# Attention with a distance bias and a two-layer network behind it: from stages with a bias matmul to one written order with a band multiply

## The chip, the core and the metric

One core of a Trainium2 chip. The metric is device time of one execution in microseconds, the median of the runs.

## What is computed

```python
scores = q @ k^T / 8 + bias_table[bucket(|i - j|)]      # 8 batches x 8 heads, 576 x 576, head size 64
attn = softmax(scores)                                  # over j
x = (attn @ v), heads side by side                      # 4608 tokens x 512
h = max(x @ w_in, 0)                                    # 512 -> 2048
out = (h * h) @ w_out                                   # 2048 -> 512
```

All inputs and the output are f32. The bucket of a distance is the distance itself below 16, grows with its logarithm from there, and is 31, the last one, from 128 on.

## The kernel before

The work runs in stages: the attention of two batches, then both layers for their 1152 tokens (`ffn`), four times. An automatic scheduler orders the instructions within what the data allow; all PSUM tiles come from one pool of four tiles of two banks.

`attention_batch` first transposes Q and K of a batch on TensorE in f32, five pieces for each pair of heads (`transpose_pair`, L162 and L165); VectorE copies them to bf16 and scales Q (L171, L173). VectorE casts V to f16 into a tile with a 65th column of 1/64 (L191 to L199), so that the row sums come out of the same matmul as the values.

The scores stand transposed: keys on the partitions, queries along the columns, in blocks of 128 keys (the fifth has 64) and 288 queries. A block gets two matmuls. The first adds the bias (L213): a reversed identity of 128 x 128 times a window of `dbuf_sb`, a table in which each partition holds the bias by distance, shifted by one (built over DRAM at the start, L129 to L144). The second adds K^T Q with the 64 rows of one head (L222). ScalarE takes the exponential of both query halves, 576 columns, to f16 (L231). Then come 10 matmuls for a head with the weights as moving operand (L241). To divide by the row sum, ScalarE takes its logarithm (L251), GpSimd spreads it over 64 partitions (L256), ScalarE takes exp(-x) (L257), and VectorE multiplies (L255, L260).

`ffn` computes layer 1 in 16 blocks of 128 hidden columns, 12 matmuls each (L277), ScalarE rectifies (L284), VectorE squares (L291). Layer 2 takes 9 token blocks of 16 matmuls of 512 columns (L297); VectorE scales them out of PSUM (L305) and SP writes them out. All loads are issued on SP's queue, those of the next batch after the casts of this one.

Of the kernel before, what the change touches and what calls it, by code (L numbers as in the profile page):

```python
# [19 lines left out]
NJT = 5  # L21
VSC = 1.0 / 64.0
OSC = 1.0 / 4096.0
EXPF = mybir.ActivationFunctionType.Exp
RELUF = mybir.ActivationFunctionType.Relu
MULT = mybir.AluOpType.mult


def _rel_bucket_diag():
    t = np.arange(1151)  # L30
    n = np.abs(t - 575)
    half = NBK // 2
    max_distance = 128
    is_small = n < half
# [5 lines left out]
    return np.where(is_small, n, large).astype(np.int64)  # L40
# [3 lines left out]
def kernel(  # L44
# [10 lines left out]
    nc = tc.nc  # L55

    bidx = _rel_bucket_diag()
    oh = np.zeros((NBK, 1280), dtype=np.float32)
    uu = np.arange(128, 128 + 1151)
    oh[bidx, uu] = 1.0  # L60
    oh_d = nc.inline_tensor(oh, name="c_oh")
    revi_d = nc.inline_tensor(
        np.eye(128, dtype=np.float32)[::-1].astype(ml_dtypes.bfloat16), name="c_revi"
    )
    id_d = nc.inline_tensor(np.eye(128, dtype=np.float32), name="c_id")
    dfull_dram = nc.dram_tensor("t_dfull", (H, 1280), BF16, kind="Internal")

    single = ctx.enter_context(tc.tile_pool(name="single", bufs=1))
    et_pool = ctx.enter_context(tc.tile_pool(name="et", bufs=12))
    qk_pool = ctx.enter_context(tc.tile_pool(name="qk", bufs=8))  # L70
    v1_pool = ctx.enter_context(tc.tile_pool(name="v1", bufs=2))
    st_pool = ctx.enter_context(tc.tile_pool(name="stg", bufs=1))
    ws_pool = ctx.enter_context(tc.tile_pool(name="ws", bufs=1))
    xt_pool = ctx.enter_context(tc.tile_pool(name="xt", bufs=2))
    sm_pool = ctx.enter_context(tc.tile_pool(name="sm", bufs=3))
    ff_pool = ctx.enter_context(tc.tile_pool(name="ff", bufs=1))
    ps = ctx.enter_context(tc.tile_pool(name="ps", bufs=4, space=bass.MemoryType.PSUM))

    id_sb = single.tile([128, 128], FP32, name="id_sb")
    revi_sb = single.tile([128, 128], BF16, name="revi_sb")  # L80
    dbuf_sb = single.tile([128, H, 1152], BF16, name="dbuf_sb")
    w_in_sb = single.tile([128, 4, 2048], FP16, name="w_in_sb")
    w_out_sb = single.tile([128, 16, 512], FP16, name="w_out_sb")
    bt_sb = single.tile([32, 16], FP32, name="bt_sb")
    gt_sb = ff_pool.tile([128, 16, 1152], FP16, name="gt_sb")

    stgs = {}

    def load_sdh(src, b, tag):
        stg = st_pool.tile([128, NJT, 512], FP32, tag=tag, name=tag)  # L90
        for tt in range(4):
            nc.sync.dma_start(
                out=stg[:, tt, :].rearrange("p (h d) -> p h d", h=8),
                in_=src[b, :, ts(tt, 128), :].transpose([1, 0, 2]),
            )
# [251 lines left out]
```

## Time and profile before

| | before |
|---|---|
| runs, us | 659.6, 654.64, 655.17 (median 655.17) |
| span of the profiled execution, first to last instruction, us | 652.9 |
| median less that span, us | 2.3 |
| TensorE, ScalarE, VectorE, GpSimd busy, us | 619.2, 342.7, 235.3, 60.6 |
| bytes read and written in HBM, MB | 39.32, 9.46 |

The profile shows one execution. Busy times are unions of instruction intervals; ends of matmuls are modelled, so distances between their starts say more than their lengths. L-numbers are lines of the kernel printed above.

### The profile page before, as it was taken

What the parts mean: (1) busy time and instruction counts of PE and PEld (TensorE: products, weight loads), DVE (VectorE), ACT (ScalarE), POOL (GpSimd) and SP (SyncE); (2) the same over time, 40 slices, a digit from 0 to 9 for tenths busy, and PEclk for the clock granted to TensorE, in tenths of its full rate; (3) what the DMA queues carried; (4) which work ended last, traced back from release to release, by engine and by line L of the source; (5) the groups of instructions that cost most, each with busy time, mean ns of one, the idle gap of its engine ahead of it and who ended that gap; (6) DMA issues with size and microseconds to landing.
All of it is one profiled execution on the core that took longest, in us unless ns stands there. A gap on an engine that the chain in (4) does not pass through costs nothing.

```text
span 652.9 us, 8868 instructions
## 1 busy us (share of the span) xinstructions
PE 619.2 (95%) x3590; PEld 296.4 (45%) x3590; DVE 235.3 (36%) x327; ACT 342.7 (52%) x581; POOL 60.6 (9%) x76
## 2 busy tenths in 40 slices
PE   6699989899999999999999999989999999999997
PEld 3244534454454444445454454445445445444543
DVE  2223644642243262433142352343324325324321
ACT  0188688561038758665007757846202785876500
POOL 0021121100002211200001211210000211220000
PEclk9999999999999999999999999989999999999999
DMA  7992767341180091030227038000016300000012
GB/s 168 252 211 89 229 206 177 73 74 48 65 167 11 1 180 41 0 73 1 81 80 130 1 69 150 1 2 2 32 67 139 53 1 1 2 0 1 1 65 81
DMA packets 122169, 49.36 MB, mean 76 GB/s; under 512 B 113768, under 2 KB 113896, under 8 KB 121616
## 3 DMA queue, kind: packets, MB, share of 16 engines
q1 hardware_dynamic: 122128, 48.79, 33.0%
q8 instruction: 28, 0.46, 0.3%
q14 instruction: 13, 0.11, 0.1%
HBM read 39.32 MB, written 9.46 MB: 75 GB/s over the span
## 4 chain that ended last, share of the span: by engine, by line
PE 52%; issue 30%; ACT 9%; POOL 3%; DVE 3%; DMA 3%; SPq 0%; POOLq 0%; ACTq 0%; DVEq 0%
PE yps L297 14%; PE hps L277 13%; PE ot L241 10%; PE st L213 6%; PE st L222 5%; ACT et L231 4%; POOL rb L256 3%; ACT rb L257 3%; ACT rl L251 2%; PE tpsk L162 1%; DVE xt L260 1%; DMA kstg<-in_k_dram 1%; PE tpsq L162 1%; DMA dbuf_sb<-t_dfull 1%; PE dfps L129 1%
## 5 line engine op out<-in xcount | busy, mean ns | idle before, releaser
L231 ACT ACTIVATE et<-st 128x576 f16<-128x576 f32 (+1 forms) x320 | 180.9, 649 | 159.3 <-PE st L222 157.9
L277 PE MATMUL hps<-xt,w_in_sb 128*128 128x512 f16 (+1 forms) x768 | 129.0, 328 | 6.9 <-DVE xt L260 2.7
L213 PE MATMUL st<-dbuf_sb,revi_sb 128*128 128x288 bf16 (+1 forms) x640 | 127.8, 293 | 5.8 <-ACT et L231 3.6
L297 PE MATMUL yps<-w_out_sb,gt_sb 128*128 128x512 f16 x576 | 125.0, 379 | 0.0
L255 DVE COPY xtr<-ot 64x576 f32<-64x576 f32 x64 | 47.9, 748 | 195.4 <-ACT rl L251 195.4
L222 PE MATMUL st<-tq,tk 64*128 64x288 bf16 (+1 forms) x640 | 110.2, 291 | 0.0
L241 PE MATMUL ot<-et,v 128*65 128x288 f16 (+1 forms) x640 | 105.5, 293 | 2.4 <-ACT et L231 1.9
L256 POOL PARTITION_BROADCAST rb<-rl x64 | 58.8, 920 | 526.4 <-ACT rl L251 526.4
L284 ACT ACTIVATE gt_sb<-hps 128x1024 f16<-128x1024 f32 (+1 forms) x128 | 75.9, 649 | 51.2 <-PE hps L277 51.2
L277 PEld LDWEIGHTS <-w_in_sb 128*128 128x128 f16 x768 | 64.9, 98 | 70.9 <-issue 8.5
L297 PEld LDWEIGHTS <-gt_sb 128*128 128x128 f16 x576 | 56.2, 98 | 67.0
L241 PEld LDWEIGHTS <-v 128*65 128x65 f16 (+1 forms) x640 | 60.5, 110 | 48.1 <-issue 39.4
L213 PEld LDWEIGHTS <-revi_sb 128*128 128x128 bf16 (+1 forms) x640 | 45.5, 100 | 68.8 <-issue 58.8
L291 DVE TENSOR_TENSOR gt_sb<-gt_sb 128x1152 f16<-128x1152 f16 x64 | 48.5, 758 | 74.9 <-ACT gt_sb L284 74.8
L251 ACT ACTIVATE rl<-ot 1x576 f32<-1x576 f32 x64 | 41.1, 643 | 56.5 <-PE ot L241 56.5
L305 DVE TENSOR_SCALAR ysb<-yps 128x512 f32<-128x512 f32 x36 | 24.9, 691 | 95.2 <-PE yps L297 95.2
L222 PEld LDWEIGHTS <-tk 64*128 64x128 bf16 (+1 forms) x640 | 30.5, 96 | 62.2 <-issue 62.2
L260 DVE TENSOR_TENSOR xt<-xtr,rb 64x576 f16<-64x576 f32 x64 | 49.6, 776 | 15.2 <-ACT rb L257 15.0
L257 ACT ACTIVATE rb<-rb 64x576 f32<-64x576 f32 x64 | 43.2, 676 | 6.5 <-POOL rb L256 6.5
L162 PE MATMUL tpsk<-id_sb,kstg 128*128 128x128 f32 x128 | 23.3, 306 | 9.8 <-DMA kstg<-in_k_dram 5.9
L173 DVE CAST tk<-tpsk 128x576 bf16<-128x576 f32 x32 | 22.9, 750 | 10.2 <-PE tpsk L165 9.8
L171 DVE TENSOR_SCALAR tq<-tpsq 128x576 bf16<-128x576 f32 x32 | 23.6, 752 | 4.9 <-PE tpsq L165 4.5
(20 smaller groups left out, 117.5 us busy)
## 6 DMA issues: line engine op xcount, KB each, us to landing
out_dram<-ysb SPq DMA_DIRECT2D x36, 256.0 KB, 2.0
qstg<-in_q_dram SPq DMA_DIRECT2D x32, 256.0 KB, 4.7
kstg<-in_k_dram SPq DMA_DIRECT2D x32, 256.0 KB, 5.3
vstg<-in_v_dram SPq DMA_DIRECT2D x32, 256.0 KB, 4.7
ws<-in_moe_w_in_dram SPq DMA_DIRECT2D x4, 1024.0 KB, 5.2
ws<-in_moe_w_out_dram SPq DMA_DIRECT2D x16, 256.0 KB, 4.6
dbuf_sb<-t_dfull SPq DMA_DIRECT2D x8, 288.0 KB, 5.1
qstg<-in_q_dram SPq DMA_DIRECT2D x8, 128.0 KB, 5.0
```

Source lines behind the costliest of these rows:

```text
L213: nc.tensor.matmul(stp[0:jw, ic, 0:IC], rv, dbuf_sb[:, 2 * hp + hd, ff0 : ff0 + IC], start=True, stop=False,)
L222: nc.tensor.matmul(sts[hd][0:jw, ic, 0:IC], kt[ds(hd * 64, 64), ts(jt, 128) if jt < 4 else ds(512, 64)], qt[ds(hd * 64, 64), ds(ic * IC, IC)],
L231: nc.scalar.activation(out=et[0:jw, :, :], in_=sts[hd][0:jw, :, 0:IC], func=EXPF)
L241: nc.tensor.matmul(ot[0:65, ic, 0:IC], v1b[0:jw, hh, jt, 0:65], ets[hd][jt][0:jw, ic, :], start=(jt == 0), stop=(jt == NJT - 1),)
L251: nc.scalar.activation(out=rl[0:1, :], in_=ot[64:65, :, 0:IC], func=mybir.ActivationFunctionType.Ln,)
L256: nc.gpsimd.partition_broadcast(rb[0:64, :], rl[0:1, :], 64)
L257: nc.scalar.activation(out=rb[0:64, :], in_=rb[0:64, :], func=EXPF, scale=-1.0,)
L260: nc.vector.tensor_tensor(out=xt[ds((hh % 2) * 64, 64), hh // 2, ds(bo * 576, 576)], in0=xtr[0:64, :], in1=rb[0:64, :], op=MULT,)
L277: nc.tensor.matmul(hps[:, mc, 0:wd], w_in_sb[:, kk, ts(nt, 128)], xt[:, kk, ds(mcb * 1024 + mc * 512, wd)], start=(kk == 0), stop=(kk == 3),)
L284: nc.scalar.activation(out=gt_sb[:, nt, ds(mcb * 1024, nmc * wd)].rearrange("p (a c) -> p a c", a=nmc), in_=hps[:, 0:nmc, 0:wd], func=RELUF,)
L291: nc.vector.tensor_tensor(out=gt_sb[:, nt, :], in0=gt_sb[:, nt, :], in1=gt_sb[:, nt, :], op=MULT)
L297: nc.tensor.matmul(yps[:, 0, :], gt_sb[:, nt, ts(mt, 128)], w_out_sb[:, nt, :], start=(nt == 0), stop=(nt == 15),)
```

## The change

Everything is written anew, and the order of the instructions is now the order of the program on every engine (`io`).

- **Pipeline.** While batch b is in the attention, layer 1 of batch b - 1 and layer 2 of batch b - 2 run in between. A batch of attention has 56 slots: 36 of scores (a block of 128 keys with two matmuls, an exponential of 576 and a band multiply), 16 of values (five matmuls), four of transposes (of the next pair of heads). After each slot comes its share of the quanta of the layers: 32 of layer 1 (four matmuls of 288 columns, one rectification), and 32 or 40 of layer 2 (two matmuls of 512). Batch 0 has no quanta. Steps behind the values are put off by a slot each (`defer`, `tick`).
- **Bias.** exp(s + bias) = exp(s) exp(bias). Beyond distance 127 the bias is that of bucket 31, which the division takes out. So VectorE multiplies the exponentials by exp(bias - bias31) within that distance only, from a table in f16 that is built at the start with eight f32 matmuls, four exponentials and a round through DRAM, issued on ScalarE's queue.
- **Keys.** K of a pair lies in one tile with zeros in the other head's 64 rows, so score matmuls have 128 rows. The last 64 keys of both heads share one block. V lies likewise in tiles of 128 columns, 64 of them 1/64, so the row sum comes out on 64 partitions, and GpSimd's broadcast goes.
- **Transposes** take f16 copies of Q and K. GpSimd makes them (VectorE and ScalarE for batch 0), as well as V's and the layers' weights'. The scale 1/8 goes into the exponential.
- **PSUM**: two tiles of two banks for scores, tables and transposes (`psS`), two single banks for values (`psP`), two for the layers (`psF`).
- Layer 1 squares 512 tokens and a tail of 64 in two instructions; the tails of two batches make a fifth block of layer 2.

```diff
+BAND = [(0, 256), (0, 384), (128, 512), (256, 576), (384, 576)]
...
+    def io(ins):
+        tc.keep_in_program_order(ins)
+        return ins
...
+    stg_pool = ctx.enter_context(tc.tile_pool(name="stg", bufs=1))
+    h16_pool = ctx.enter_context(tc.tile_pool(name="h16", bufs=1))
+    ws_pool = ctx.enter_context(tc.tile_pool(name="ws", bufs=2))
+    qt_pool = ctx.enter_context(tc.tile_pool(name="qt", bufs=3))
+    et_pool = ctx.enter_context(tc.tile_pool(name="et", bufs=16))
+    nr_pool = ctx.enter_context(tc.tile_pool(name="nr", bufs=2))
+    rt_pool = ctx.enter_context(tc.tile_pool(name="rt", bufs=3))
+    gt_pool = ctx.enter_context(tc.tile_pool(name="gt", bufs=2))
+    y_pool = ctx.enter_context(tc.tile_pool(name="y", bufs=2))
+    psS = ctx.enter_context(tc.tile_pool(name="psS", bufs=2, space=bass.MemoryType.PSUM))
+    psP = ctx.enter_context(tc.tile_pool(name="psP", bufs=1, space=bass.MemoryType.PSUM))
+    psF = ctx.enter_context(tc.tile_pool(name="psF", bufs=2, space=bass.MemoryType.PSUM))
...
+    kzs = [single.tile([128, 2 * S], FP16, name=f"kz{i}") for i in range(3)]
+    vzs = [single.tile([128, 5, H, 128], FP16, name=f"vz{i}") for i in range(2)]
...
+        if by_head:
+            for h in range(H):
+                for t, src in ((qs, q), (ks, k)):
+                    sdma(
+                        nc.sync,
+                        t[:, 0:4, ts(h, 64)],
+                        src[b, h, 0:512, :].rearrange("(t p) d -> p t d", p=128),
+                    )
+                if h == 1:
+                    tail(qs, q)
+                    tail(ks, k)
+        else:
...
+    def cast_qk(b):
+        qh = h16_pool.tile([128, 5, 512], FP16, tag="qh", name="qh")
+        kh = h16_pool.tile([128, 5, 512], FP16, tag="kh", name="kh")
+        h16[b] = (qh, kh)
+        qs, ks, _ = stgs[b]
+        if b == 0:
+            for hp in range(4):
+                io(nc.vector.tensor_copy(out=qh[:, 0:4, ts(hp, 128)], in_=qs[:, 0:4, ts(hp, 128)]))
+                io(nc.scalar.activation(out=kh[:, 0:4, ts(hp, 128)], in_=ks[:, 0:4, ts(hp, 128)], func=COPYF))
+                if hp == 0:
+                    io(nc.vector.tensor_copy(out=qh[0:64, 4, :], in_=qs[0:64, 4, :]))
+                    io(nc.scalar.activation(out=kh[0:64, 4, :], in_=ks[0:64, 4, :], func=COPYF))
+        else:
+            for dst, src in ((qh, qs), (kh, ks)):
+                io(nc.gpsimd.tensor_copy(out=dst[:, 0:4, :], in_=src[:, 0:4, :]))
+                io(nc.gpsimd.tensor_copy(out=dst[0:64, 4, :], in_=src[0:64, 4, :]))
+    def cast_v(b):
+        vz, vs = vzs[b % 2], stgs[b][2]
+        for e in range(2):
+            o = 64 * e
+            for t0, t1, p0, p1 in ((0, 4, 0, 128), (4, 5, o, o + 64)):
+                io(
+                    nc.gpsimd.tensor_copy(
+                        out=vz[p0:p1, t0:t1, e::2, o : o + 64],
+                        in_=vs[p0:p1, t0:t1, :].rearrange(
+                            "p t (h e d) -> p t h e d", e=2, d=64
+                        )[:, :, :, e, :],
+                    )
...
+    def weights(src, dst, n, w):
+        for kk in range(n):
+            if w > 1024:
+                for c in range(0, w, 1024):
+                    s_ = ws_pool.tile([128, 1024], FP32, tag="ws", name="ws")
+                    sdma(nc.sync, s_, src[ts(kk, 128), c : c + 1024])
+                    io(nc.gpsimd.tensor_copy(out=dst[:, kk, c : c + 1024], in_=s_))
...
+    def setup_tables():
+        io(nc.vector.tensor_copy(out=btb_sb, in_=bt_sb.unsqueeze(2).to_broadcast([32, H, 128])))
+        te = gt_pool.tile([128, H, 512], FP16, tag="g", name="te")
+        for h2 in range(4):
+            tp = psS.tile([128, 2, 512], FP32, tag="s", name="tp")
+            for e in range(2):
+                io(nc.tensor.matmul(tp[:, e, :], btb_sb[:, 2 * h2 + e, :], oh_sb, start=True, stop=True))
+            io(nc.scalar.activation(out=te[:, 2 * h2 : 2 * h2 + 2, :], in_=tp, func=EXPF))
+        sdma(nc.scalar, tdram.ap(), te)
+        pitch = H * 512 - 1
+        sdma(
+            nc.scalar,
+            tb_sb,
+            bass.AP(tensor=tdram, offset=128, ap=[[pitch, 128], [512, H], [1, 384]]),
...
+    def transposes(p):
+        b, hp = divmod(p, 4)
+        qh, kh = h16[b]
+        tp = psS.tile([128, 2, 1024], FP16, tag="s", name="tp")
+        for w, src, pieces in (
+            (0, qh, [(tt, 128 * tt) for tt in range(5)]),
+            (1, kh, [(4, 0)] + [(tt, 64 + 128 * tt) for tt in range(5)]),
+        ):
+            for tt, c in pieces:
+                n = 128 if tt < 4 else 64
+                io(
+                    nc.tensor.transpose(
+                        tp[:, w, ds(c, n)],
+                        src[0:n, tt, ts(hp, 128)],
+                        id_sb[0:n, 0:n],
+                    )
+                )
+        qt = qt_pool.tile([128, S], FP16, tag="qt", name="qt")
+        kz = kzs[p % 3]
+        io(nc.vector.tensor_copy(out=qt, in_=tp[:, 0, 0:S]))
+        io(nc.vector.tensor_copy(out=kz[0:64, 0:S], in_=tp[0:64, 1, 64 : 64 + S]))
+        io(nc.vector.tensor_copy(out=kz[64:128, S : 2 * S], in_=tp[64:128, 1, 0:S]))
+        qts[p] = (qt, kz)
+    def scores(p, jt, ic):
+        qt, kz = qts[p]
+        hp = p % 4
+        st = psS.tile([128, 2, 512], FP32, tag="s", name="st")
+        for e in range(2):
+            if jt < 4:
+                lhs, c0 = kz[:, ds(640 * e + jt * 128, 128)], ic * IC
+            else:
+                lhs, c0 = kz[:, 512:640], e * IC
+            io(nc.tensor.matmul(st[:, e, 0:IC], lhs, qt[:, ds(c0, IC)], start=True, stop=True))
+        et = et_pool.tile([128, 2, IC], FP16, tag="et", name="et")
+        io(nc.scalar.activation(out=et, in_=st[:, :, 0:IC], func=EXPF, scale=SCALE))
+        lo, hi = BAND[jt]
+        if jt < 4:
+            a, z = max(lo, ic * IC), min(hi, ic * IC + IC)
+            if a < z:
+                sl = et[:, :, a - ic * IC : z - ic * IC]
+                w0 = a - jt * 128 + 128
+                io(
+                    nc.vector.tensor_tensor(
+                        out=sl, in0=sl, in1=tb_sb[:, 2 * hp : 2 * hp + 2, w0 : w0 + z - a], op=MULT
+                    )
...
+    def tick():
+        for x in later:
+            x[0] -= 1
+        while later and later[0][0] <= 0:
+            later.popleft()[1]()
+    def pv(p, ic):
+        b, hp = divmod(p, 4)
+        vz = vzs[b % 2]
+        if (hp, ic) == (0, 0):
+            xts[b] = xt_pool.tile([128, 4, S], FP16, tag="xt", name="xt")
+        xt = xts[b]
+        pvs = [psP.tile([128, 512], FP32, tag=f"p{e}", name=f"pv{e}") for e in range(2)]
+        for e in range(2):
+            for jt in range(5):
+                rhs = ets[p, jt, ic][:, e, :] if jt < 4 else ets[p, 4, 0][:, ic, :]
+                io(
+                    nc.tensor.matmul(
+                        pvs[e][:, 0:IC], vz[:, jt, 2 * hp + e, :], rhs, start=(jt == 0), stop=(jt == 4)
+                    )
+                )
+            if e == 0:
+                yield
+        r = nr_pool.tile([128, IC], FP32, tag="r", name="r")
+        io(nc.scalar.activation(out=r[0:64, :], in_=pvs[0][64:128, 0:IC], func=LNF))
+        io(nc.scalar.activation(out=r[64:128, :], in_=pvs[1][0:64, 0:IC], func=LNF))
+        def fin1():
+            io(nc.scalar.activation(out=r, in_=r, func=EXPF, scale=-1.0))
+            def fin2():
+                for e in range(2):
+                    o = 64 * e
+                    io(
+                        nc.vector.tensor_tensor(
+                            out=xt[o : o + 64, hp, ds(ic * IC, IC)],
+                            in0=pvs[e][o : o + 64, 0:IC],
+                            in1=r[o : o + 64, :],
+                            op=MULT,
+                        )
+                    )
+                if (hp, ic) == (3, 1):
+                    ready.add(b)
+            defer(1, fin2)
+        defer(1, fin1)
...
+            rt = rt_pool.tile([128, S], FP16, tag="rt", name="rt")
+            for ic in range(2):
+                hps = psF.tile([128, 512], FP32, tag="f", name="hps")
+                for kk in range(4):
...
+                io(nc.scalar.activation(out=rt[:, ts(ic, IC)], in_=hps[:, 0:IC], func=RELUF))
+                if ic == 1:
+                    m0 = 0 if b % 2 == 0 else 64
+                    t0 = 512 if b % 2 == 0 else 0
+                    o = 64 * (b % 2)
+                    io(
+                        nc.vector.tensor_tensor(
+                            out=g[:, nt, :], in0=rt[:, ds(m0, 512)], in1=rt[:, ds(m0, 512)], op=MULT
+                        )
+                    )
...
+    def ffn2(b):
+        tiles = [(gts[b], ts(m, 128), b * S + 64 * (b % 2) + m * 128) for m in range(4)]
+        if b % 2 == 1:
+            tiles.insert(0, (gtails[b // 2], slice(0, 128), b * S - 64))
+        for g, sl, row in tiles:
+            yps = psF.tile([128, 512], FP32, tag="f", name="yps")
+    def mixed(b1, b2):
+        f1 = ffn1(b1) if 0 <= b1 < B else iter(())
+        f2 = ffn2(b2) if 0 <= b2 < B else iter(())
+        n2 = (4 + b2 % 2) if 0 <= b2 < B else 0
+        n1 = 32 if 0 <= b1 < B else 0
+        done1 = 0
+        for y in range(max(n2, 1)):
+            for _ in range(8 if n2 else 0):
+                next(f2)
+                yield
+            upto = n1 * (y + 1) // max(n2, 1)
+            while done1 < upto:
+                assert b1 in ready
+                next(f1)
+                done1 += 1
+                yield
+        for f in (f1, f2):
...
+    load(0, by_head=True)
...
+    setup_tables()
+    cast_qk(0)
+    cast_v(0)
+    weights(moe_w_in, w_in_sb, 4, 2048)
+    transposes(0)
...
+        if b + 1 < B:
+            load(b + 1)
+            cast_qk(b + 1) if b > 0 else None
+        slots = []
+        for hp in range(4):
+            p = 4 * b + hp
+            for ic in range(2):
+                early = (hp, ic) == (0, 0)
+                slots.append(("s", p, 0, ic))
+                slots.append(("pv",)) if early else None
+                slots.append(("s", p, 1, ic))
+                slots.append(("pv",))
+                slots.append(("s", p, 2, ic))
+                slots.append(("s", p, 3, ic))
+                slots.append(("pv",)) if not early else None
+                if ic == 0:
+                    slots.append(("s", p, 4, 0))
+                else:
+                    slots.append(("t", p + 1))
+                slots.append(("end", p, ic))
+        n_real = sum(s_[0] != "end" for s_ in slots)
+        done, at = 0, 0
+        skip = 0 if b >= 2 else 8
+        for s_ in slots:
+            if s_[0] == "end":
+                nxt = pv(s_[1], s_[2])
+                pending = nxt
+                continue
+            if s_[0] == "s":
+                scores(*s_[1:])
+            elif s_[0] == "t":
+                if s_[1] < 4 * B:
+                    if b == 0 and s_[1] == 4:
+                        cast_qk(1)
+                    transposes(s_[1])
+            elif pending is not None:
+                next(pending, None)
+            at += 1
+            while done < total * max(at - skip, 0) // (n_real - skip):
+                next(fq)
+                done += 1
+            tick()
+        for _ in fq:
+            raise AssertionError
+        if b + 1 < B:
+            cast_v(b + 1)
         if b == 0:
...
+            weights(moe_w_out, w_out_sb, 16, 512)
```

## Rows read from the trace of the kernel before

**Rows 1.** The page, part 1: busy us (share of the span) of each engine.

```profile
PE 619.2 (95%) x3590; PEld 296.4 (45%) x3590; DVE 235.3 (36%) x327; ACT 342.7 (52%) x581; POOL 60.6 (9%) x76
```

**Rows 2.** Timeline of TensorE in the attention of batch 2: start, duration, form, count.

```profile
200.25 0.41 PE L222 MATMUL st<-tq,tk 64*128 64x288 bf16 x2
200.59 0.42 PE L213 MATMUL st<-dbuf_sb,revi_sb 128*128 128x288 bf16 x2
200.95 0.41 PE L222 MATMUL st<-tq,tk 64*128 64x288 bf16 x2
...
203.44 3.23 PE L241 MATMUL ot<-et,v 128*65 128x288 f16 x20
```

**Rows 3.** Timeline of TensorE, 203.58 to 204.4: first matmuls of the values alone.

```profile
203.44 1.17 PE L241 MATMUL ot<-et,v 128*65 128x288 f16 x8
```

**Rows 4.** Groups by line and form: busy us, mean ns, idle before.

```profile
L231 ACT ACTIVATE et<-st 128x576 f16<-128x576 f32 x256 | 145.6, 648 | 159.1 <-PE st L222 157.9
...
L284 ACT ACTIVATE gt_sb<-hps 128x1024 f16<-128x1024 f32 x64 | 65.6, 1024 | 51.2 <-PE hps L277 51.2
...
L291 DVE TENSOR_TENSOR gt_sb<-gt_sb 128x1152 f16<-128x1152 f16 x64 | 48.5, 758 | 74.9 <-ACT gt_sb L284 74.8
...
L305 DVE TENSOR_SCALAR ysb<-yps 128x512 f32<-128x512 f32 x36 | 24.9, 691 | 95.2 <-PE yps L297 95.2
...
L191 DVE CAST v<-vstg 128x2048 f16<-128x2048 f32 x8 | 10.7, 1337 | 1.8 <-DMA vstg<-in_v_dram 1.8
```

**Rows 5.** Timeline of TensorE, transposes of batch 2: two starts of a group of five.

```profile
182.03 0.66 PE L162 MATMUL tpsq<-id_sb,qstg 128*128 128x128 f32 x4
182.62 0.27 PE L165 MATMUL tpsq<-id_sb,qstg 64*128 64x64 f32 x1
182.82 0.66 PE L162 MATMUL tpsq<-id_sb,qstg 128*128 128x128 f32 x4
```

**Rows 6.** Timeline of TensorE, layer 2 of the first two batches.

```profile
150.22 31.24 PE L297 MATMUL yps<-w_out_sb,gt_sb 128*128 128x512 f16 x144
```

**Rows 7.** Timeline of ScalarE: two blocks of layer 1; eight exponentials in a line.

```profile
126.80 1.19 ACT L284 ACTIVATE gt_sb<-hps 128x1024 f16<-128x1024 f32 x2 [0.76 <-PE hps L277]
128.75 1.19 ACT L284 ACTIVATE gt_sb<-hps 128x1024 f16<-128x1024 f32 x2 [0.76 <-PE hps L277]
...
199.76 4.43 ACT L231 ACTIVATE et<-st 128x576 f16<-128x576 f32 x8
```

**Rows 8.** Timeline of VectorE: copies out of PSUM without a wait between them.

```profile
228.06 0.74 DVE L260 TENSOR_TENSOR xt<-xtr,rb 64x576 f16<-64x576 f32 x1
228.73 0.74 DVE L255 COPY xtr<-ot 64x576 f32<-64x576 f32 x1
229.40 0.74 DVE L171 TENSOR_SCALAR tq<-tpsq 128x576 bf16<-128x576 f32 x1
```

**Rows 9.** Timeline of VectorE and GpSimd at 428.6; the line of the broadcast (min/median/max ns).

```profile
428.67 1.53 DVE L191 CAST v<-vstg 128x2048 f16<-128x2048 f32 x1
...
429.08 1.83 POOL L256 PARTITION_BROADCAST rb<-rl  x1
430.12 1.26 DVE L260 TENSOR_TENSOR xt<-xtr,rb 64x576 f16<-64x576 f32 x1
...
L256 POOL PARTITION_BROADCAST rb<-rl x64: 855/859/1830, 37.1 to 586.7; - x64
```

**Rows 10.** Windows: length, busy us of each engine, granted clock of TensorE, DMA.

```profile
433.00:437.00 4.00, 3.00 (x10) 1.20 (x10) 1.68 (x3) 2.28 (x4) 0.00 (x0) 0.72 0.02 6
```

**Rows 11.** Chain of waits at the start: start, us, what.

```profile
5.06 4.43 PE dfps L129 x6
...
9.96 1.55 DMA t_dfull<-dfull_sb
...
26.80 0.64 PE st L213 x2
...
28.03 0.59 PE st L213 x2
```

**Rows 12.** DMA issues: KB each, median us to landing.

```profile
qstg<-in_q_dram SPq DMA_DIRECT2D x32, 256.0 KB, 4.7
...
ws<-in_moe_w_in_dram SPq DMA_DIRECT2D x4, 1024.0 KB, 5.2
```

**Rows 13.** Timeline of VectorE at the end.

```profile
649.13 0.69 DVE L305 TENSOR_SCALAR ysb<-yps 128x512 f32<-128x512 f32 x1 [2.76 <-PE yps L297]
```

More of the change, by code (lines that the diff above doesn't have):

```diff
@@ L2 @@
+from collections import deque
 from contextlib import ExitStack
@@ L39, in _rel_bucket_diag @@
     large = np.minimum(large, NBK - 1)
[L40 removed]
+    return np.where(n < half, n, large).astype(np.int64)
 @with_exitstack
@@ L77 @@
[L77 to L81, printed above, removed]
+    assert (_bucket(np.arange(128, S)) == NBK - 1).all()
+    def io(ins):
+        tc.keep_in_program_order(ins)
+        return ins
+    oh = np.zeros((NBK, 512), dtype=np.float32)
+    oh[_bucket(np.abs(np.arange(512) - 256)), np.arange(512)] += 1.0
@@ L159, in transpose_pair @@
-    def transpose_pair(stg, hp, sc, nm):
-        tps = ps.tile([128, 2, 512], FP32, tag="ps", name="tps" + nm)
-        for tt in range(4):
-            nc.tensor.transpose(
-                tps[:, 0, ts(tt, 128)], stg[:, tt, ts(hp, 128)], id_sb[:, :]
-            )
-        nc.tensor.transpose(
-            tps[:, 1, 0:64], stg[0:64, 4, ts(hp, 128)], id_sb[0:64, 0:64]
-        )
-        tsb = qk_pool.tile([128, 576], BF16, tag="qkt", name="t" + nm)
-        flat = tps.rearrange("p a b -> p (a b)")[:, 0:576]
-        if sc:
-            nc.vector.tensor_scalar_mul(out=tsb, in0=flat, scalar1=SCALE)
-        else:
-            nc.vector.tensor_copy(out=tsb, in_=flat)
-        return tsb
@@ L268, in ffn @@
-    def ffn(bp):
-        xt = xts[bp]
-        for nt in range(16):
-            for mcb in range(2):
-                hps = ps.tile([128, 2, 512], FP32, tag="ps", name="hps")
-                nmc = 2 if mcb == 0 else 1
-                wd = 512 if mcb == 0 else 128
-                for kk in range(4):
-                    for mc in range(nmc):
-                        nc.tensor.matmul(
-                            hps[:, mc, 0:wd],
+            sdma(
+                nc.sync,
+                vs[:, tt, :].rearrange("p (h d) -> p h d", h=8),
+                v[b, :, ts(tt, 128), :].transpose([1, 0, 2]),
+            )
@@ new lines, in ffn1 @@
+                yield
[5 more added lines that the diff above has]
+            yps = psF.tile([128, 512], FP32, tag="f", name="yps")
+            for nt in range(16):
+                io(nc.tensor.matmul(yps, g[:, nt, sl], w_out_sb[:, nt, :], start=(nt == 0), stop=(nt == 15)))
+                if nt == 15:
+                    y = y_pool.tile([128, 512], FP32, tag="y", name="y")
+                    io(nc.vector.tensor_scalar_mul(out=y, in0=yps, scalar1=OSC))
+                    sdma(nc.sync, out[ds(row, 128), :], y)
+                if nt % 2 == 1:
+                    yield
```

341 lines of the change are left out of this document (133 added, 208 removed).

## Prediction

> **What bounds the kernel now.** I read the engines' shares first: TensorE is busy in 95% of the span, ScalarE in 52%, VectorE in 36% [rows 1]. But ends of matmuls are modelled, so I went to the timeline of TensorE and took distances between starts. In the attention, matmuls stand in pairs: two with 128 rows, two with 64 (form 128\*128, then 64\*128), a pair each 0.34 to 0.36 us, 0.175 a matmul of 288 columns [rows 2]. Eight with 128 rows in a line take 0.126 each ((1.17 − 0.29)/7) [rows 3], and the rate of layer 2, 31.24 us for 144 of 512 columns [rows 6], gives 0.122 for 288. So each change between 64 and 128 rows costs 0.35 − 2 × 0.122 = 0.106 us. The 20 matmuls of weights times values, with some changes, take 3.23 us, 0.155 each [rows 2].
>
> Does this make up the span? Scores 1280 × 0.175 = 224; values 640 × 0.155 = 99; layer 1, whose ScalarE rhythm is 1.95 us per block of 128 hidden columns, 64 × 1.95 = 125 [rows 7]; layer 2 576 × 0.217 = 125; transposes 64 × 0.79 = 50.6 (one group of five starts 0.79 after the one before) [rows 5], of which batch 0's 6.3 lie ahead of the first score at 26.8 [rows 11]. 26.8 + 224 + 99 + 125 + 125 + 44 = 644, and the last eviction starts at 649.1 [rows 13]. The rest is some 5 us of waits: the kernel is TensorE's own work, stage after stage.
>
> **Part by part: TensorE's work.** Bias matmuls go; the last 64 keys of two heads share a matmul; keys are padded to 128 rows. That leaves 18 instead of 40 score matmuls per head pair, all with 128 rows: 576 × 0.122 = 70. Values: 640, all 128 rows: 78. Layer 1 has the same columns, now 1024 × 0.122 = 125. Layer 2: 125. Transposes are 11 per pair, 8 full and 3 of 64 rows with 4 changes. The trace has no 16-bit transpose: from below the column rate of an f16 matmul, 8 × 0.055 + 3 × 0.03 + 4 × 0.106 = 0.95; from above the f32 pace, 2.2 groups × 0.79 = 1.74. I take 1.0, by the f16 rows: 32. Sum 430, against 624.
>
> **The start.** The first score waits for a new chain: both tables' inputs (the old matmul starts at 5.06 [rows 11]), 8 f32 table matmuls at 1.7 (2.5 of them took 4.43) = 13.6, an exponential of 1.0 [rows 4], table write 1.55, then reading it back and the casts of K, both on ScalarE's queue behind a wait for that write: 0.8 + 1.3; transposes 1 to 2, copies 2. That is 27 to 28; I take 28, 22 if the matmuls run at the higher clock level, 34 if the table write lands late. The early matmuls do run slow: pairs 0.59 apart at 28 us [rows 11] against 0.35 later, so the lower of the two levels (1.2 against 2.4 GHz).
>
> With the end of 3.8 (652.9 − 649.1), and one transpose group ahead of the first score: 28 + 429 + 4 = **461** without waits.
>
> **New waits.** TensorE, ScalarE and VectorE now run in one written order with two score buffers, one pair of value buffers and two for the layers.
>
> (a) Transposes of the next head pair stand in the last slot, right ahead of its first scores. Those need three VectorE copies; behind the waiting TensorE is all the rest of its queue. Cover is one slot's share of layer work: 64 or 72 quanta over 56 slots, 1.2 × 0.46 = 0.55 (0.49 for four matmuls of 288, 0.43 for two of 512). An f32 copy out of PSUM follows its neighbour by 0.67 [rows 8]; 16-bit operands on both sides take half per element (1152 in 0.758 against 512 in 0.691 [rows 4]), 0.48 ns beside a fixed 0.2, of which 0.08 overlaps the neighbour: 0.40 for 576. Three copies: 1.2 to 2.0; the f16 tile in PSUM resembles one row by place, the other by width, so 1.65. Wait 0.1 + 1.65 − 0.55 = 1.2, and 1.75 in batch 0, which has no cover: 28 × 1.2 + 4 × 1.75 = **41** (26 to 52). The Trainium skill, "VectorE: DVE Perf Modes", section "The perf-mode tier table (the rule you actually need)", lets a copy from PSUM reach twice the single rate; no row here shows it on PSUM, and by it the term would be 26.
>
> (b) Batch 0 has no layer work. ScalarE's exponentials follow each other by 0.54 ((4.43 − 0.65)/7) [rows 7], and one of 288 by 0.30 (slope 0.84 ns from 576 and 1024 [rows 4], less an overlap of 0.11). 9 × 0.54 + 6 × 0.30 = 6.7 a pair, beside TensorE's 5.6 + 1.75; the chain from one value group to the next (two logarithms, exp, a score's exp, its band multiply, two multiplies out of PSUM) is 2.5 us against some 1.6 of scores: 1 us × 8. Then Q and K of batch 1: on SP's queue they are behind 4 MB of layer-1 weights that pass through two buffers and GpSimd's casts (1 MB lands in 5.2, 256 KB in 4.7 [rows 12]), so they land near 55 and are cast by 61, when TensorE wants them: 0 to 8, I take 3. **12** (4 to 25).
>
> (c) Batches 1 to 7. The same chain, with layer work in ScalarE's queue, is 3.1 us, against three score slots and four shares of layer work, 2.95: 0.2 × 28 = 6. While layer 1 runs, a score slot costs ScalarE 0.54 + 1.2 × 0.30 = 0.90 and TensorE 0.244 + 1.2 × 0.49 = 0.83; each layer-1 buffer is free again about 0.9 after its last matmul (behind an exponential in ScalarE's queue), with 0.98 of cover. I take 0.08 for 256 quanta: 20. GpSimd now casts 7,680 elements a partition each batch, its own queue holding batch b + 1's Q behind the last transposes of batch b: by VectorE's cast 0.65 ns each, by the broadcast of 576 in 0.86 1.5 ns [rows 4, 9], 5 to 11 us. It fits into the 15 us of a pair, but VectorE and GpSimd hold each other up: the cast of 1.34 on average took 1.53 beside a broadcast, that broadcast 1.83 instead of 0.86, the next multiply 1.26 [rows 9]. One transposition per batch lies there: 1 us × 7. **33** (0 to 70). At nothing I cost what SP and GpSimd do besides: layer 2's weights (4 MB more, some 20 us on both queues) are wanted a whole batch later, without which each buffer would cost its 5 us; outputs stand on SP behind the loads of batch b + 1, the last of which, V, waits for GpSimd's cast of V early in the batch, while two output buffers cover two tiles of 3.45 each. The Trainium skill, "SBUF — State Buffer", section "Who interferes with whom", says a VectorE instruction with two SBUF inputs and a GpSimd one that reads SBUF exclude each other for a whole instruction; the three rows agree.
>
> (d) Last value group before the last layers: **4**.
>
> The load of the others doesn't bound: ScalarE 288 × 0.54 + 448 × 0.30 = 290; VectorE 256 band multiplies 76 (92,160 elements × 0.48 ns + 0.12 each), 128 multiplies out of PSUM 51, 128 squares with their tails 67, 96 copies 53, 36 evictions 22: 269.
>
> Sum 461 + 41 + 12 + 33 + 4 = **551** of span. The median of the runs, 655.17, is 2.3 above the profiled span: 553.
>
> **The rivals.**
> - Copies at the 16-bit rate and waits that swallow each other (a TensorE that waits lets the others catch up): a 26, b 8, c 10, d 3, 508 + 2 = 510. For it: loads of 270 to 290 beside 430. Against: only two buffers. The Trainium skill's rule on copies from PSUM, above, would by itself give 15 less than the forecast.
> - VectorE behind GpSimd: each long cast holds band multiplies, squares and, queued behind, the copies, and layer 1 stops when three rectified tiles are full. At the upper price 11 us a batch are exclusive; 8 us of them on TensorE instead of 1 adds 49: 602. For it: [rows 9]; against: these fall into a quarter of the batch. The Trainium skill's rule on the shared SBUF interface, above, is this one.
> - The change doesn't do what it says: spacing came from something else than the rows, and 128-row scores and values stay at 0.175 and 0.155: 576 × 0.053 + 640 × 0.033 = 52 more, 605. Against: [rows 3].
> - Slower: TensorE at 1.2 GHz. After a stretch with waits (433 to 437) the granted clock averages 0.72 [rows 10], and the first score pairs run at half the pace. With waits in every pair the lower level could last. It doubles TensorE's work: past (655 + 7 − 553)/430 = 25% of it at the lower level the kernel is slower. At a third: 553 + 143 = 696. Against: only this one stretch in the middle of the old run shows the lower level, behind several waits in a row, and in 3.4 us it was over.
>
> **How the numbers follow.** Forecast (525 to 580) 0.48; fast rival 0.22; GpSimd 0.12 and unchanged spacing 0.04, both near 603; worse sums of the same waits up to 648 0.04; slower by over 1% 0.07; within 1%, which is about what this measurement can tell from nothing, 0.03. All but the last two are faster: 0.90. The range leaves out the best tenth below the fast rival's 510 (its own lower bounds, a 26, b 4, c 0, give 495) and about a tenth above: 495 to 612.
>
> **What would show it.** In the changed trace: score and value matmuls 0.122 apart with one form 128\*128 (else the third rival); after each transposition TensorE idle about 1.2 us, released by a copy (a); copies of 0.4 or 0.67 spacing; first score near 28; VectorE instructions stretched while GpSimd casts; granted clock near 1 from batch 1. The prediction falls if ScalarE or VectorE is busy over 80% of batches 2 to 7, so that one of them sets the pace, if the transposition of batch 1 waits over 10 us for its casts, or if the clock stays low.

## The result, and the profile after

The changed kernel takes 560.6 us (559.29 to 563.36, 4 runs) against 654.9 in the runs beside it: ratio 0.855, interval 0.850 to 0.859. The forecast was 553, in a range of 495 to 612. The profiled execution took 559.29, with a span of 557.5. One execution of experiment 1 below took 1186.82 us, where its other three took 534.0 to 534.4, and is left out.

The shares come first [rows 1]. TensorE lost 136 us of busy time and is still what everything waits for; VectorE gained 78.

```profile
PE 482.7 (87%) x3184; PEld 304.5 (55%) x3184; DVE 313.7 (56%) x781; ACT 350.3 (63%) x746; POOL 83.0 (15%) x90
```

TensorE's timeline in batch 2 (start, duration, form, count) answers to [rows 2, 3, 5]: one form of rows for scores, layer 1 and values, five values in 0.62 us (150.01 to 150.63), 0.124 each, and eleven 16-bit transposes. Layer 2 keeps its rate [rows 6]: 80 matmuls in 17.43 us at the end of the chain of waits.

```profile
149.28 0.41 PE L263 MATMUL st<-qt,kz 128*128 128x288 f16 x2
149.52 0.65 PE L353 MATMUL hps<-xt,w_in_sb 128*128 128x288 f16 x4
150.01 0.78 PE L307 MATMUL pv<-et,vz 128*128 128x288 f16 x5
150.63 0.65 PE L353 MATMUL hps<-xt,w_in_sb 128*128 128x288 f16 x4
151.12 0.52 PE L240 MATMUL tp<-id_sb,qh 128*128 128x128 f16 x5
151.47 0.65 PE L240 MATMUL tp<-id_sb,kh 64*128 64x64 f16 x6
```

The chain of waits has the start [rows 11], long VectorE instructions in every batch from 1 to 6, of which three are shown, and layer 2 at its end (start, us, what):

```profile
4.43 14.00 PE tp L205 x16
19.51 3.88 DMA t_bias<-te
...
166.30 1.76 DVE g L367
168.06 2.91 DVE gtail L372
232.00 1.79 DVE gtail L372
...
536.24 17.43 PE yps L388 x80
```

The groups by line and form answer to [rows 4, 8]: exponentials as before, rectifications 414 ns, copies out of PSUM 0.44 to 0.46 us. A square of a 64-column tail, 0.19 us where nothing disturbs it, is 336 ns in the mean.

```profile
L265 ACT ACTIVATE et<-st 128x576 f16<-128x576 f32 x288 | 183.6, 650 | 105.2 <-PE st L263 104.3
...
L361 ACT ACTIVATE rt<-hps 128x288 f16<-128x288 f32 x256 | 105.4, 414 | 55.1 <-PE hps L353 47.8 <-issue 2.6 <-ACT rt L361 0.6
...
L372 DVE TENSOR_TENSOR gtail<-rt 128x64 f16<-128x64 f16 x128 | 43.0, 336 | 0.0
...
L250 DVE COPY kz<-tp 64x576 f16<-64x576 f16 x32 | 14.7, 461 | 1.0
...
L248 DVE COPY qt<-tp 128x576 f16<-128x576 f16 x32 | 14.6, 456 | 23.9 <-PE tp L240 23.4
L249 DVE COPY kz<-tp 64x576 f16<-64x576 f16 x32 | 14.1, 440 | 0.0
```

Two stretches say what went otherwise than forecast. The first is the timeline of VectorE, GpSimd and the next score at the end of batch 2 (the bracket is the idle time before it and its releaser), which answers to [rows 9]:

```profile
165.89 1.89 POOL L165 CAST qh<-qs 128x2048 f16<-128x2048 f32 x1 [53.78 <-PE tp L240]
...
166.30 1.76 DVE L367 TENSOR_TENSOR g<-rt 128x512 f16<-128x512 f16 x1 [1.14 <-ACT rt L361]
...
167.73 0.80 POOL L166 CAST qh<-qs 64x512 f16<-64x512 f32 x1
167.99 2.99 DVE L372 TENSOR_TENSOR gtail<-rt 128x64 f16<-128x64 f16 x1
168.48 1.89 POOL L165 CAST kh<-ks 128x2048 f16<-128x2048 f32 x1
170.32 0.61 POOL L166 CAST kh<-ks 64x512 f16<-64x512 f32 x1
170.88 2.90 POOL L174 CAST vz<-vs 128x1024 f16<-128x1024 f32 x4
171.00 0.46 DVE L248 COPY qt<-tp 128x576 f16<-128x576 f16 x1
171.38 0.44 DVE L249 COPY kz<-tp 64x576 f16<-64x576 f16 x1
...
171.88 0.91 PE L263 MATMUL st<-qt,kz 128*128 128x288 f16 x2 [4.53 <-DVE kz L249]
```

GpSimd waited 53.78 us for this batch's last transposes, then ran Q, K and V in one line. The square ends just after Q's large cast; the tail waits until K's casts are over. Behind it on VectorE's queue stand the copies that TensorE needs. The second is the window after it (length, busy us of PE, PEld, DVE, ACT, POOL, granted clock, DMA), which answers to [rows 10]: the lower level, 1.2 GHz, for 6.8 us.

```profile
169.80:176.60 6.80, 4.66 (x15) 2.20 (x16) 5.63 (x10) 1.30 (x2) 3.92 (x6) 0.50 0.01 2
234.60:238.00 3.40, 3.21 (x12) 1.71 (x13) 3.34 (x4) 1.78 (x4) 3.40 (x4) 0.50 0.00 0
```

Six such stretches lie between 64 and 430 us, 34.0 in sum. All but the first follow a transposition held up in this way.

For the accounts below I took the distance from each matmul's start to the next, less 0.4215 ns per column (0.2158 us for 512 columns of layer 2) and 0.1 us where the rows change. In the six stretches up to as much again per column is put down to the clock; the rest is put down to the matmul that waited.

### The profile page after: what moved, and what is told of

The parts are those of the page before. It is cut to its first block, busy times and chain, and to the rows that moved or that the text cites. A ratio compares the mean times of both kernels' runs of the same rounds, so it can differ in the third digit from the quotient of the medians.

```text
span 557.5 us, 8693 instructions
## 1 busy us (share of the span) xinstructions
PE 482.7 (87%) x3184; PEld 304.5 (55%) x3184; DVE 313.7 (56%) x781; ACT 350.3 (63%) x746; POOL 83.0 (15%) x90
## 4 chain that ended last, share of the span: by engine, by line
PE 66%; DVE 18%; ACT 11%; issue 3%; DMA 1%; ACTq 0%; DVEq 0%
PE yps L388 20%; PE hps L353 17%; PE pv L307 14%; PE st L263 10%; ACT et L265 4%; DVE gtail L372 4%; PE tp L240 3%; ACT rt L361 3%; DVE g L367 3%; DVE kz L250 3%; PE tp L205 3%; DVE kz L249 2%; DVE y L391 2%; DVE qt L248 2%; DVE xt L324 2%
## 5 line engine op out<-in xcount | busy, mean ns | idle before, releaser
L265 ACT ACTIVATE et<-st 128x576 f16<-128x576 f32 x288 | 183.6, 650 | 105.2 <-PE st L263 104.3
L353 PE MATMUL hps<-xt,w_in_sb 128*128 128x288 f16 x1024 | 163.0, 288 | 4.8 <-ACT rt L361 2.7
L263 PE MATMUL st<-qt,kz 128*128 128x288 f16 x576 | 126.6, 298 | 46.2 <-DVE kz L249 31.2
L388 PE MATMUL yps<-w_out_sb,g 128*128 128x512 f16 x512 | 140.8, 387 | 0.0
L361 ACT ACTIVATE rt<-hps 128x288 f16<-128x288 f32 x256 | 105.4, 414 | 55.1 <-PE hps L353 47.8
L273 DVE TENSOR_TENSOR et<-et,tb_sb 128x576 f16<-128x576 f16 (+5 forms) x224 | 82.8, 376 | 93.4 <-ACT et L265 89.7
L307 PE MATMUL pv<-et,vz 128*128 128x288 f16 x640 | 103.8, 295 | 8.1 <-DVE xt L324 8.1
L367 DVE TENSOR_TENSOR g<-rt 128x512 f16<-128x512 f16 x128 | 64.7, 505 | 46.2 <-ACT rt L361 44.2
L307 PEld LDWEIGHTS <-vz 128*128 128x128 f16 x640 | 64.4, 101 | 40.4 <-issue 14.3
L324 DVE TENSOR_TENSOR xt<-pv,r 64x288 f16<-64x288 f32 x128 | 58.1, 454 | 5.4 <-ACT r L318 1.9
```

Source lines behind the costliest of these rows:

```text
L263: io(nc.tensor.matmul(st[:, e, 0:IC], lhs, qt[:, ds(c0, IC)], start=True, stop=True))
L265: io(nc.scalar.activation(out=et, in_=st[:, :, 0:IC], func=EXPF, scale=SCALE))
L273: nc.vector.tensor_tensor(out=sl, in0=sl, in1=tb_sb[:, 2 * hp : 2 * hp + 2, w0 : w0 + z - a], op=MULT)
L307: nc.tensor.matmul(pvs[e][:, 0:IC], vz[:, jt, 2 * hp + e, :], rhs, start=(jt == 0), stop=(jt == 4))
L324: nc.vector.tensor_tensor(out=xt[o : o + 64, hp, ds(ic * IC, IC)], in0=pvs[e][o : o + 64, 0:IC], in1=r[o : o + 64, :], op=MULT,)
L353: nc.tensor.matmul(hps[:, 0:IC], w_in_sb[:, kk, ts(nt, 128)], xt[:, kk, ds(ic * IC, IC)], start=(kk == 0), stop=(kk == 3),)
```

## Experiments

**1. How long GpSimd's casts are** (`e1_small_casts`; `e1b_small_casts` is a second run of the same kernel, and its trace is the one that is read).

```diff
-  io(nc.gpsimd.tensor_copy(out=dst[:, 0:4, :], in_=src[:, 0:4, :]))
+  for hp in range(4):
+      io(nc.gpsimd.tensor_copy(out=dst[:, 0:4, ts(hp, 128)], in_=src[:, 0:4, ts(hp, 128)]))
```

> GpSimd's two casts of 2048 elements for Q and K of the next batch become eight of 512. Theory A (a VectorE instruction with two SBUF inputs waits for one whole GpSimd instruction, then gets its turn): the longest VectorE square falls from 2.9 us to some 0.9, TensorE's wait behind the transposes of a batch's last head pair from 4.7 to under 2, and the stretches at the lower clock that follow go: 7 x 3 + 8 = 30 us less, 530. Theory B (instructions of GpSimd that stand back to back keep the interface from one to the next): squares and waits stay within 0.5 us, 555 to 565. Theory C (the copies are late for another reason, VectorE's own load): within 4 us of the changed kernel.

> The kernel of e1 once more, for its trace. If theory A carries the 26 us that it gained: no VectorE instruction longer than about 1.3 us while GpSimd casts, TensorE's waits behind the transposes of a batch's last head pair 1 to 2 us instead of 4.7, granted clock back at 0.99. If VectorE still stands for 3 us and more, the gain came from elsewhere.

534.3 us, ratio 0.813 (0.809 to 0.817), and 534.48: 26 us less than the changed kernel for the same elements cast by the same engine. Batches 2 to 6 take 58.0 and 60.3 us by turns, in place of 63.0 to 63.3. In the waits (us in total, times, longest) of TensorE this kernel shows, for the copy that the first score needs:

```profile
PE st L264 <- DVE kz L250: 14.5, 25, 2.4
```

in place of this in the changed kernel:

```profile
PE st L263 <- DVE kz L249: 31.2, 25, 5.6
```

The lower clock is left in two stretches of 3.4 us. The gain is near theory A's 30, but its turn after one cast did not come: VectorE gets in after one to three casts, and its longest instruction while GpSimd casts is 2.41 (a band multiply at 167.56), not 0.9 or 1.3.

**2. Pieces, spread over the batch** (`e2_spread_casts`): each head pair's Q and K are cast in place, one transposition after the one that read them; V's casts stay at the end.

```diff
-  h16[b] = (qh, kh)
+  h16[b] = qh, kh = h16[0]
...
   transposes(s_[1])
+  if s_[1] % 4 and b + 1 < B:
+      cast_qk(b + 1, s_[1] % 4 - 1)
```

> The casts of Q and K of the next batch are cut by head pair, and each piece is written into the place that the transposes of the same head pair of this batch have just read; so two short casts stand behind each of the transposes instead of ten us of work behind the last ones. Theories A and B both: no VectorE instruction waits over 1.2 us, TensorE's 4.7 us waits and the lower clock behind them go, 30 to 35 us less, 525 to 530. Theory C (not the casts): within 4 us. If each head pair now pays a little of the interface (0.5 us x 28), 540.

569.7, ratio 0.867 (0.863 to 0.871): slower than the changed kernel, and a miss for all three theories. The pieces are as small as in experiment 1, but they and V's still stand in a line, and one square stands beside eight of them (it starts as the first ends, and ends within the last):

```profile
170.65 0.85 POOL L169 CAST qh<-qs 128x512 f16<-128x512 f32 x2 [13.05 <-PE tp L243]
171.25 3.63 DVE L370 TENSOR_TENSOR g<-rt 128x512 f16<-128x512 f16 x1 [1.14 <-ACT rt L364]
171.44 0.85 POOL L169 CAST kh<-ks 128x512 f16<-128x512 f32 x2
172.24 2.90 POOL L177 CAST vz<-vs 128x1024 f16<-128x1024 f32 x4
```

So a short cast is no protection by itself.

**3. Another engine for the casts.** `e5_gp_spaced`, `e6_vector_casts` and `e7_scalar_casts` write one piece after each slot, on GpSimd, VectorE or ScalarE. In all three, batch 2's Q and K were cast over those of batch 1 before batch 1's head pairs 1 to 3 were transposed, so these pairs are computed from batch 2's, and TensorE waits 17 to 23 us for that; only batches 2 to 6 are read. `e9_vector_casts` is `e6_vector_casts` with its own tiles for batches 1 and 2 (in both, VectorE casts those of batches 3 to 7).

```diff
+  for t0, t1, n in ((0, 4, 128), (4, 5, 64)):
+      todo.append(lambda ...: io(nc.vector.tensor_copy(out=dst[0:n, t0:t1, c], in_=src[0:n, t0:t1, c])))
...
   tick()
+  if todo:
+      todo.popleft()()
```

> From batch 2 on the casts of the next batch's Q, K and V stay on GpSimd but one short piece stands behind each slot, none back to back with another. In the spread version before, a square waited 3.6 us through eight casts in a row. If rows of GpSimd instructions are what holds VectorE: longest VectorE instruction near 1 us, lower clock gone from batch 2 on, 15 to 25 us less than the changed kernel (the first two batches keep their casts), 535 to 545. If each cast costs its length wherever it stands: 36 of 0.3 to 1.0 us a batch spread the same loss, 555 to 565.

> The same pieces in the same slots on VectorE, GpSimd idle from batch 2 on. If the shared interface is the cause: no stretched VectorE instruction, 20 to 25 us less, 535 to 540; VectorE has 6 us a batch more to do, of 62. If VectorE's own load is what makes the copies late: slower than the changed kernel, 565 or more.

> The same pieces on ScalarE, which has its own access. 9 us a batch more on ScalarE beside 42 of 62. If the interface is the cause and ScalarE has room: 535 to 545. If ScalarE's queue is as tight as the prediction's term c took it (a score slot 0.90 on ScalarE against 0.83 on TensorE while layer 1 runs): the gain is eaten, 555 to 570.

> Casts of Q, K and V for batches 3 to 7 in pieces of a head pair, one after each slot, on VectorE in place of GpSimd; batches 0 to 2 as in the changed kernel, whole GpSimd casts with them. Theory (the stretched VectorE instructions and the lower clock behind them come from GpSimd's casts standing beside VectorE's work): in batches 2 to 6 no VectorE instruction over 1.6 us, no stretch at the lower clock, 57 to 60 us a batch in place of 63.1, 560.6 - 5 x 4.6 = 537, near the 534 of the small casts on GpSimd. Rival (VectorE's own extra load, some 6 us a batch, makes new waits): over 550.

GpSimd, in pieces: 63.6 to 65.5 us a batch (whole kernel 585.2, 0.893, 0.887 to 0.899), so neither of its theories was tested. The places in the program don't space them: nothing ties GpSimd to the slots, so four pieces again run within 1.7 us as soon as the transposes are done (232.92 to 234.57 in its trace), and the squares take 592 and 308 ns in the mean. ScalarE: 59.7 and 62 to 63.7 (569.0, 0.867, 0.864 to 0.871); it is now busy 85% of a batch (50.55 of 59.67 us in batch 2), and layer 1 waits 2.8 us per batch in place of 1.0 to 1.5. VectorE: 57.0 and 59.9, in `e6` (554.1, 0.844, 0.840 to 0.848) as in `e9` (536.7, 0.818, 0.814 to 0.822). A window of `e9`, from the first score of batch 3 to that of batch 4, has the clock at 1.00, and the lines of VectorE between 182 and 417 us have its squares at their own length:

```profile
182.54:242.48 59.94, 57.60 (x404) 37.43 (x405) 39.42 (x118) 42.52 (x93) 0.00 (x0) 1.00 0.40 76
...
L376 DVE TENSOR_TENSOR g<-rt 128x512 f16<-128x512 f16 x65 | 27.5, 423 | 16.8 <-ACT rt L370 15.4
...
L381 DVE TENSOR_TENSOR gtail<-rt 128x64 f16<-128x64 f16 x64 | 11.8, 184 | 0.0
L176 DVE CAST qh<-qs 128x512 f16<-128x512 f32 (+1 forms) x32 | 10.2, 318 | 0.4
```

The same lines in the changed kernel have 508 and 316 for the squares. VectorE does the casts besides (318 ns each) and the batch still gets 3 to 6 us shorter: what cost was not the load but the two engines side by side. Where GpSimd still casts, at the end of batch 1, `e9` keeps the wait of 5.63 us and the 6.8 us at the lower clock.

**4. The transposes two slots earlier** (`e3_t_earlier`).

```diff
   slots.append(("s", p, 2, ic))
-  slots.append(("s", p, 3, ic))
-  slots.append(("pv",)) if not early else None
   if ic == 0:
+      slots.append(("s", p, 3, ic))
+      slots.append(("pv",)) if not early else None
       slots.append(("s", p, 4, 0))
   else:
       slots.append(("t", p + 1))
+      slots.append(("pv",))
+      slots.append(("s", p, 3, ic))
```

> Transposes of the next head pair stand two slots earlier, ahead of the second value slot and the last score slot. Theory (prediction's term a): TensorE waits for the three copies because only one slot's share of work covers them; now 2.5 us cover them. The waits of 0.6 to 1.6 us per head pair (some 30 us in all, without those behind the casts) go to near 0, and the waits behind GpSimd's casts shrink by 2 each: 30 to 40 us less, 520 to 530. Rival: they are handed on, to the chain of the value tiles or to the score buffers, which stand as tight: less than 10 us gained.

559.1, ratio 0.851 (0.846 to 0.856): no change. Waits ahead of scores fall from 61 to 36 us; those ahead of values rise from 12.8 to 28.5, of layer 1 from 11.9 to 15.7, of layer 2 from 0.5 to 5.4, and the stretched squares stay. The rival held: VectorE's copies come earlier, and something else of VectorE's later.

**5. 64-row scores** (`e4_rows64`): the first four key blocks contract over one head's 64 rows, as before.

```diff
-  lhs, c0 = kz[:, ds(640 * e + jt * 128, 128)], ic * IC
+  r = ds(64 * e, 64)
+  lhs, rhs = kz[r, ds(S * e + jt * 128, 128)], qt[r, ds(ic * IC, IC)]
```

> Padding undone for the first four key blocks: each score matmul takes the 64 rows of its head instead of 128 with zeros (the fifth block stays). Theory (each change between 64 and 128 rows costs 0.106 us): 256 score slots with two changes each are 54 us of TensorE, a part of it inside waits that are there anyway: 40 to 55 us more, 600 to 615. Rival 1 (two matmuls with different 64 rows run at once): faster, down to 535. Rival 2 (the old spacing came from the bias matmuls or the type): no change, 558 to 565.

581.0, ratio 0.885 (0.881 to 0.889), 20 us slower than the changed kernel, where the theory gave 40 to 55. From the last 128-row matmul ahead of such a pair to the first behind it the starts show 0.312 + 0.003 + 0.225, where 0.216 + 0.122 + 0.122 stood: both changes of rows cost 0.1, but the second of the pair starts 3 ns after the first, so rival 1 held in part and gives 0.12 back. With 0.01 more at the next matmul a slot takes 0.335 in place of 0.244. Of the 256 slots 212 stand alone between 128-row matmuls, and these make 19 us. The stretches at the lower clock are 65 us long here, in place of 34, so how much of the 20 us is rows alone is not shown.

**6. The order alone** (`e8_stages`): the same instructions, but a batch's quanta of both layers stand behind its attention.

```diff
-  while done < total * max(at - skip, 0) // (n_real - skip):
-      next(fq)
-      done += 1
   tick()
   for _ in fq:
-      raise AssertionError
+      pass
```

> The same instructions, but the quanta of both layers of a batch stand behind all its attention slots instead of between them; nothing else changes. Theory (the pipeline's gain is that the layers' matmuls cover the wait behind transposes and the chain of ScalarE and VectorE between groups of values): batches 1 to 7 then run their attention at the pace of batch 0, 40.5 us, in place of 63.1 less some 31 of layers = 32, so 7 x 8 = 56 more, 615, and with the layers alone, whose pace ScalarE may set (32 rectifications and 16 squares per batch), not under 600. Rival (most of the gain is the matmuls that went, and TensorE catches up elsewhere): under 575. In the first case the share of the old time that the order alone is worth is read from the difference.

636.8, ratio 0.972 (0.967 to 0.978): 76 us slower than the changed kernel, where the theory gave 56. So 76 of the 94 us hang on the order; without it, some 200 us less work on TensorE are worth 18. By the account of starts (in an execution of 644.39) TensorE's work is the same 425, and its waits and the lower clock take 184 us in place of 97. The waits of TensorE in its trace name the largest: scores wait for ScalarE's exponentials, two buffers being all there are, and values for VectorE.

```profile
PE st L263 <- ACT et L265: 46.9, 41, 1.5
...
PE pv L307 <- DVE xt L324: 18.3, 24, 1.8
```

In the changed kernel these are 9.1 and 8.1 us.

**7. The start** (`e10_start`): the table is read back behind the casts of K on ScalarE's queue.

```diff
   sdma(nc.scalar, tdram.ap(), te)
+  def read_tables(): ...
   setup_tables()
   cast_qk(0)
+  read_tables()
```

> One move: the reads of the bias table back from DRAM stand behind the casts of batch 0's K on ScalarE's queue instead of ahead of them. Theory (the first score waits for ScalarE's queue, which stands 5.8 us behind the table's write): K cast by 21, first score at 23 to 24 instead of 28.3, 556. Rival (the band multiplies need the table anyway, so the wait only moves to the first values): first score earlier, but the start of batch 1 at 68.8 as before or under 2 us earlier, 559 to 561.

559.2, ratio 0.852 (0.848 to 0.856): no change. The first score starts at 23.18 in place of 28.32, as expected, but ScalarE then stands 5.11 us at the read, the scores wait 4.07 behind its first two exponentials, and batch 1 starts at 67.69 in place of 68.80. The rival held.

**8. Together** (`e11_both`): experiments 3 and 7, VectorE's casts from batch 2 on, GpSimd's of batch 1 in pieces. The edits are the ones shown there and in experiment 1.

> Together: VectorE casts in pieces for batches 2 to 7, GpSimd's casts of batch 1 in pieces of a head pair, and the reads of the table behind K's casts. Theory (the waits are apart, so the gains add): batches 1 to 6 at 55 to 60 us, first score at 23 to 24, 560.6 - 7 x 4.6 - 4 = 524. Rival (part of one is the other's cover): 530 to 536, no faster than small GpSimd casts alone.

543.4, ratio 0.828 (0.825 to 0.831), a miss for theory and rival. From batch 2 on it has 57.0 and 59.9 as `e9`, but batch 1 takes 65.0 us: its VectorE stood for Q and K of batch 2, which had not landed, and the values behind waited.

```profile
91.24 0.43 DVE L177 CAST qh<-qs 128x512 f16<-128x512 f32 x1 [7.28 <-DMA qs<-in_q_dram]
...
97.06 0.43 DVE L177 CAST kh<-ks 128x512 f16<-128x512 f32 x1 [4.32 <-DMA ks<-in_k_dram]
...
99.52 0.88 PE L319 MATMUL pv<-et,vz 128*128 128x288 f16 x3 [9.79 <-DVE xt L336]
```

In the changed kernel it was GpSimd that stood at such places, with nothing queued behind that TensorE needs. No version is faster than that of experiment 1; `e9` is as fast within the intervals.

## Why the prediction was right, and where its sum was not

| term, us | forecast | measured |
|---|---|---|
| TensorE's work | 430 | 425: scores 69.9, values 77.7, layers 124.3 and 124.1, transposes 29.2 |
| first score at | 28 | 28.32 |
| (a) behind transposes | 41 | 25 |
| (b) batch 0 | 12 | 12.2 |
| (c) chain between values, with (d) | 6 + 4 | 14.8 |
| (c) layer 1 | 20 | 12.4, with 0.5 of layer 2 |
| (c) VectorE beside GpSimd | 7 | 19.9 of waits; lower clock 11.4 |
| small gaps | 0 | 4 |

TensorE's work was right because it was read from distances between starts. Experiment 5 shows the price of a change of rows, 0.1, by itself, so the rival of unchanged spacing is out; undoing the padding of the keys cost 20 us. None of the three signs of being wrong came: in batches 2 to 6 VectorE is busy 38.7 and ScalarE 42.8 of 63.2 us in the mean, the transposition of batch 1 waited 0.98, and the clock of these batches was 0.95 to 1.00.

Two terms that came out were luck in part. In **the start** the table's write took 3.88 us and not 1.55, and issuing the reads 1.75 and not 0.8; against that the transposes of K took 0.97 and the two copies that the first score waits for 0.87, where 3 to 4 was put down for both. In **(b)** the parts put down, 8 and 3, make 11 and not 12. The 3 for the casts of batch 1's Q and K did not come, but up to 36.5 us the matmuls start 0.24 apart, which is some 3 of the 12.2.

**(a)** was mis-sized at the step "I take 1.65" for three copies. They took 1.3 (starts at 171.00, 171.38 and 171.85 above, then 0.46): the f16 tile in PSUM behaved by its width and not by its place. With 1.3 the wait is 0.5 to 0.9 in most batches and 1.35 in batch 0. The Trainium skill, "VectorE: DVE Perf Modes", section "The perf-mode tier table (the rule you actually need)", had it: a copy from PSUM may reach twice the single rate. The trace agrees, and the term came out at 25, near the 26 that it gives.

**(c)** hid two errors of opposite sign. The chain and layer 1 come to 27 as against 30. The interface was forecast as "1 us × 7". In the trace, the waits at each batch's last transposition, less what the same place shows in `e9` (for batch 1, what batch 0 shows), are 4.5, 4.0, 1.7, 4.0, 1.7 and 4.0 in batches 1 to 6: 19.9. The step that failed is that one hold-up was priced, as [rows 9] show one. GpSimd's casts stand in a line here, VectorE loses the hand-over from one to the next more than once, and all three copies are queued behind. The clock then falls for 3.4 or 6.8 us in all of these batches but the fifth, which no term of the sum had; the rival with the low clock had it, at a size of a third of the work. Experiments 1 and 3 (`e9`) measure both together at 26 and 24 us. The Trainium skill, "SBUF — State Buffer", section "Who interferes with whom", says that the loser is blocked for the other's whole instruction; here it was blocked for several, 2.99 us beside casts of 0.80, 1.89 and 0.61.

So the rival of VectorE behind GpSimd had the mechanism right and its price, 49 us more, too high; the fast rival had the copies right, and its waits that swallow each other wrong: experiment 4 shows them handed on. 553 against 560.6 is 16 too much in (a) and 24 too little at the interface with its clock, with small terms between. That these nearly cancel is luck.

**Open:** at which hand-overs VectorE loses. The casts of experiments 1 and 2 are of the same size, and it waits 2.4 us at most in the one and 3.63 in the other. Why these waits bring 3.4 us of lower clock at some places, 6.8 at others and none in batch 5, whose wait is the 1.7 of batch 3, was not tried either.

## What to carry to other kernels

Price two engines that hold each other up by all that stands in a line on the other, then by what is queued behind the one held, and then by the clock after. Removing work from the busiest engine pays only as far as something of its own is written into each wait: here the removed matmuls alone were worth 18 us, and with the order 94. The new order with the old matmuls was not tried; it had only some 5 us of waits to fill. Move a cast onto an engine that can afford to stand while its input has not landed (experiment 8).

## What was not expected of the hardware

- VectorE's copies out of PSUM kept 0.44 to 0.46 us beside GpSimd's casts (171.00, above), while its instructions with two inputs in SBUF were stretched. Two inputs do not seem to be a condition, though: at the start a cast of Q, with one, took 2.17 us beside GpSimd's memsets, and 0.43 when they were over. The cast in [rows 9] has one input as well.

```profile
5.51 2.17 DVE L158 CAST qh<-qs 128x512 f16<-128x512 f32 x1 [1.50 <-DMA qs<-in_q_dram]
5.55 0.96 POOL L438 MEMSET vz<- 128x1024 f16 x1
...
6.44 0.96 POOL L439 MEMSET vz<- 128x1024 f16 x1
...
9.30 0.43 DVE L158 CAST qh<-qs 128x512 f16<-128x512 f32 x1 [1.11 <-DMA qs<-in_q_dram]
```

- Two matmuls of 64 rows on different halves start 3 ns apart (151.934 and 151.937 in experiment 5), and the gain is lost in the changes of rows around them.
- By the account a third of the interface's price came after the waits: behind 4.5 us without matmuls 6.8 us at 1.2 GHz, in sum 9.9 of 29.8 us (batch 0's 1.5 left out). It isn't always paid on top: batch 3 has 3.4 us at the lower clock and batch 5 none, and both take 63.3 us, because batch 3's values wait 1.3 us and batch 5's 2.6.
